# LSH attention with spectral token mixing on Trainium2: q and k handed over transposed, and split without TensorE transposes

## The chip, the cores and the metric

The kernel runs on one core of one Trainium2 chip. The metric is device microseconds of one execution; smaller is better. The kernel before took 851.65 us (median of three runs, 851.07 to 852.93).

## The reference

Two stages follow each other. The first is attention restricted by hash buckets: q and k (4 batches, 8 heads, 768 tokens, 64 dimensions) are projected on 6 random directions, the 6 signs make a bucket number, and a query sees the keys of its own bucket only. The second mixes tokens and channels.

```python
q_bits = (np.einsum('bhsd,dk->bhsk', q, proj) > 0).astype(np.int64)
k_bits = (np.einsum('bhsd,dk->bhsk', k, proj) > 0).astype(np.int64)
mask = q_bucket[:, :, :, None] == k_bucket[:, :, None, :]
scores = scale * np.matmul(q, k.transpose(0, 1, 3, 2))
scores = np.where(mask, scores, -1000000000.0)
scores = scores - np.max(scores, axis=-1, keepdims=True)
attn = np.exp(scores)
attn = attn / (np.sum(attn, axis=-1, keepdims=True) + 1e-09)
x = np.matmul(attn, v)            # then heads side by side: (4, 768, 512)

theta = x @ w_theta
zr, zi = x * np.cos(theta), x * np.sin(theta)
u = x + np.einsum('ts,bsd->btd', w_tok_r, zr) + np.einsum('ts,bsd->btd', w_tok_i, zi)
out = u + np.maximum(u @ w_ch, 0.0)
```

All inputs and the output are float32 as far as this change is concerned.

## The kernel before

**Tokens and tiles.** 768 tokens are 6 blocks of 128. Token p x 6 + t lies on partition p of block t. Two heads (64 dimensions each) share the 128 partitions of a tile, so there are 16 head pairs, four for each batch. The kernel counts attention in 96 steps: 4 batches x 8 heads x 3.

**Precision.** A float32 value is kept as a high half, rounded for TensorE (type fp32r), and a low half, the remainder. `prep_qk` (L562) makes both for q and k of a head pair. It loads the two inputs with tokens on partitions into two tiles nat (L572, two transfers each, one for each head, in pieces of 64 floats). TensorE turns each block of 128 x 128 against the identity (L592); four results fill one shared PSUM bank, pt. From there ScalarE writes the high half into hl (L597) and VectorE the low half (L600). That happens three times for a head pair, with 12 transposes.

**What follows in the head pair.** TensorE multiplies the halves with the split projection (pb, L76), and VectorE turns signs into rows (L626). `assemble` (L665) copies halves and sign rows by DMA from hl and rows into qt and kt (L672 to L681); a score is then the product of 108 rows of the first plane and 97 of the second. The first head of the run is assembled by copies on ScalarE and VectorE instead (L630, L648, L650). `maxima` (L697) computes a first approximation of all scores (sq), VectorE reduces the row maxima (mc, L723), and the row of shifts goes to qt by DMA.

**The step.** For each chunk of 512 scores TensorE computes st, ScalarE the exponential pf (L801) and its 16-bit high part p (L807), GpSimd the remainder (L813, pf minus p), and TensorE multiplies both with the two halves of v into po. VectorE divides and writes x (L856, L862). `prep_v` (L439) prepares the halves of v, for which VectorE and GpSimd read vb (L486 to L493).

**The mixing.** `moe` (L870) runs for a batch beside the attention of the next: x is transposed and split (pt_x, h_x, l_x; L907 to L916), multiplied with w_theta (ps_th), turned to sine and cosine on ScalarE (L973, L974), multiplied with x (f, L985), split into 16-bit halves (L990 to L996), multiplied with the token weights (py), added to x (L1024), transposed and split again (pt_u), multiplied with w_ch (ps_r) and stored (L1031, L1034). The weights are prepared during batch 0: `widened` (L349) and `prep_wtok` (L402), which transposes the token weights (pwt, L424).

**What sets the order.** Each piece of work is an `Op` with a rank (`prio`), the engines that may do it, each with an assumed cost, the operations that it needs, and its slots. `issue_all` (L111) simulates the engines with these costs and writes out one program for each engine: a free engine takes the ready operation of lowest rank, but leaves it alone if one that ranks ahead by more than AHEAD will be ready within HOLD of its duration. Ranks are the step plus a constant: the load of a head pair has QKL, the transposes and splits QK0, the sign products QK1, assembling AS0, the maxima MX0 and MX1, the mixing TH0, TH1, Y0, Y1, YS. Constants with `_0` or `_3` hold for the first or last batch. Where an operation may run on two engines (L996: GpSimd or VectorE), the simulated state decides. All DMAs are issued by SyncE in one queue, in the planned order.

**PSUM.** Eight banks: two for maxima (mx), two for scores (s) and four shared ones (m), for pt, pb, po, the weight transposes and all of the mixing.

Of the kernel before, what the change touches and what calls it, by code (L numbers as in the profile page):

```python
# [14 lines left out]
F32 = mybir.dt.float32  # L15
# [16 lines left out]
def lsh_attention_moe_kernel(ctx: ExitStack, tc: tile.TileContext, q, k, v, proj, w_theta, w_tok_r, w_tok_i, w_ch, aff, out):  # L32
    nc = tc.nc
    PE, ACT, DVE, POOL = nc.tensor, nc.scalar, nc.vector, nc.gpsimd

    B, H, S, D = q.shape
    NB = proj.shape[1]
# [43 lines left out]
    START = {"PE": 1000, "ACT": 1900, "DVE": 1600, "POOL": 2300, "SP": 500}  # L81
    STREAM = {"qktr": 0.5, "xtr": 0.5, "wtr": 0.5, "mtr": 0.3, "vall": 0.3, "vmean": 0.5, "pv": 0.83, "pv4": 0.25, "y": 1.0, "proj": 0.97}
    LAT = {"PE": 220, "ACT": 120, "DVE": 115, "POOL": 140}
# [355 lines left out]
    def prep_v(b, hp, prio):  # L439
        t = {}  # L440
        sv, sm_, sa = Slot("vv"), Slot("m"), Slot("m")
        full = t["full"] = b * NP + hp in FULL
        svb = Slot("vb")
# [50 lines left out]

        def whole(e):
            def go():
                t["vv"] = ap_.tile([P, 2, T, W1], F32, tag=sv.tag, bufs=1, name=f"vw_{b}_{hp}")
                t["vf"] = t["vv"].rearrange("p h t w -> p (h t) w")
                if e == "ACT":
                    ACT.activation(t["vf"][:, :, :D], src(), AF.Copy, scale=sc)  # L500
                else:
                    DVE.tensor_scalar(t["vf"][:, :, :D], src(), sc, None, ALU.mult)
            return go

        def ones_whole():
            POOL.memset(t["vf"][:, :, D : D + 1], ONE)

        def mean():
# [25 lines left out]
        r = op("vscale", prio, on("DVE", 460, scale), [r])  # L534
        if full:
            l1 = a = op("vw", prio, {"ACT": (830, whole("ACT")), "DVE": (480, whole("DVE"))}, [r], [svb, sv])
            o1 = op("vones", prio, on("POOL", 110, ones_whole), [a], [sv])
        else:
            a = op("vv1", prio, on("ACT", 830, high), [r], [svb, sv])
            o1 = op("vones", prio, on("POOL", 110, ones), [a], [sv])  # L540
            l1 = op("vv2", prio, on("DVE", 930, low), [a], [svb, sv])
        b_ = op("va1", prio, on("POOL", 970, s1), [l1], [svb])
# [19 lines left out]
    def prep_qk(b, hp, G, g):  # L562
        t = {}
        sh, sr = Slot("hl"), Slot("rows")
        nats = []
        for i, src in enumerate((q, k)):
            sn = Slot("nat")

            def load(i=i, src=src, sn=sn):
                t["nat", i] = nat = ap_.tile([P, T, 2, D], F32, tag=sn.tag, bufs=1, name=f"nat{i}_{b}_{hp}")  # L570
                for j in range(2):
                    dma(nat[:, :, j, :], src[b, 2 * hp + j].rearrange("(p t) d -> p t d", t=T))  # L572

            nats.append((op("qkload", G + QKL + 0.02 * i, on("SP", [(625, 2.5 * S * D * 4)] * 2, load), slots=[sn]), sn))

        def hf(c):
            return t["hl"][:, c].rearrange("p i n -> p (i n)")

        pr = G + at("QK0", b)
        TC = 4  # L580
        hs, ls = [], []
        for c0 in range(0, 2 * T, TC):
            def chunk(c0=c0):
                sm_ = Slot("m")
                u = {}
                cs = slice(c0 * P, (c0 + TC) * P)

                def tr():
                    u["pt"] = bank(sm_, [P, TC * P], f"pt_{b}_{hp}_{c0}")
                    for n in range(TC):  # L590
                        i, tt = divmod(c0 + n, T)
                        PE.transpose(u["pt"][:, ts(n, P)], t["nat", i][:, tt].rearrange("p h d -> p (h d)"), ident)  # L592

                def high():
                    if "hl" not in t:
                        t["hl"] = ap_.tile([P, 2, 2, S], F32R, tag=sh.tag, bufs=1, name=f"hl_{b}_{hp}")
                    ACT.activation(hf(0)[:, cs], u["pt"], AF.Copy)  # L597

                def low():
                    DVE.tensor_tensor(hf(1)[:, cs], u["pt"], hf(0)[:, cs].bitcast(F32), ALU.subtract)  # L600

                n0, n1 = c0 // T, (c0 + TC - 1) // T
                a = op("qktr", pr, on("PE", 109 * TC, tr), [nats[i][0] for i in range(n0, n1 + 1)], [nats[i][1] for i in range(n0, n1 + 1)] + [sm_])
                hs.append(op("qkh", pr, on("ACT", 495, high), [a], [sm_, sh]))
                ls.append(op("qkl", pr, on("DVE", 600, low), [hs[-1]], [sm_, sh]))

            chunk()

# [158 lines left out]
    def step(g, b, h, blk, mxt, vt, piece):  # L767
# [15 lines left out]
        for c in range(nc_):  # L783
            def chunk(c=c):
# [30 lines left out]
                def pv():  # L815
                    if "acc" not in t:
                        t["acc"] = bank(sm_, [P, T, W1], f"po_{nm}")
                    vv, mt = vt["vv"], vt["mt"]
                    for qi in range(ni):
                        o = t["acc"][:, i0 + qi]  # L820
                        if c == 0:
                            mm(o, mxt["ft"][:, ts(i0 + qi, P)], mt[:, j, :], begin and qi == 0, False)
                        for n in range(kc):
                            tt, col = c * kc + n, ds(n * ni * P + qi * P, P)
                            if vt["full"]:
                                mm(o, u["pf"][:, col], vv[:, j, tt], False, tt == T - 1)
                                continue
# [220 lines left out]
    g = 0  # L1048
# [24 lines left out]
ORD = 1  # L1073
FULL = ()
PSUM = (("mx", 2), ("s", 2), ("m", 4))
# [5 lines left out]
WIN = {"m": 3, "tmp": 3}  # L1081
MX0 = -3.274
MX1 = 0.377
PIECES = [{1: (0, 3)}, {0: (0, 2), 1: (2, 3)}]
PF = 0.16
KA = 0.3
KB = 0.629
KV = 0.583
KN = 0.872
AB = -0.02  # L1090
WTH = 16.607
WTS = 1.058
WC = 28.159
WCS = 0.722
# [6 lines left out]
SEED = 162248  # L1101
TH0_3 = -1.231
TH1_3 = 0.851
Y0_3 = 9.278
YS_3 = 6.0
Y1_3 = 2.611
MX0_0 = -3.0
MX1_0 = 0.377
AS0_0 = -5.618
PV0_0 = -4.074  # L1110
QK0_0 = -6.17
QK1_0 = -5.94
HOLD = 0.3
LATE = 6
WL0 = 22.0
WLS = 3.0
TH0_0 = 0
TH1_0 = 0.82
Y0_0 = 8.904
Y1_0 = 2.702  # L1120
YS_0 = 6.16
AHEAD = 2.0
QKL = -8.933
QK0 = -6.006
QK1 = -5.0
AS0 = -2.867
PV0 = -4.114
LV0 = -4.311
W0 = 0.4
WS = 3.097  # L1130
TH0 = 0.0
TH1 = 0.82
Y0 = 8.904
YS = 6.16
Y1 = 2.702

# [42 lines left out]
```

## Time and profile before

| | |
|---|---|
| timed runs | 851.07, 851.65, 852.93 us |
| span of the profiled execution | 852.6 us |
| instructions | 18177 |
| mean granted TensorE clock | 0.971 |
| DMA | 79350 packets, 79.03 MB |
| GpSimd, remainder p (L813) | 288 operations, 345.4 us |

For the profiled execution the profile gives its span, from the first to the last instruction; that is the time of that execution as far as it can be seen, and it lies inside the range of the timed runs. A line of a group reads: line, engine, operation, output and inputs, shape, count; then busy time in us and the mean of one in ns; then the idle time of the engine just before, and whose end ended it. PE is a matmul or transpose, PEld the loading of its weights, DVE is VectorE, ACT ScalarE, POOL GpSimd, SP SyncE. Matmuls overlap, so a count times the mean is more than the busy time. In a row of stretches stand the stretch, its length, the busy time of each engine with its number of instructions, the granted clock (1.00 is full), the busy share of the DMA engines and GB/s. In the slices, one digit is a fortieth of the span, in tenths.

### The profile page before, as it was taken

What the parts mean: (1) busy time and instruction counts of PE and PEld (TensorE: products, weight loads), DVE (VectorE), ACT (ScalarE), POOL (GpSimd) and SP (SyncE); (2) the same over time, 40 slices, a digit from 0 to 9 for tenths busy, and PEclk for the clock granted to TensorE, in tenths of its full rate; (3) what the DMA queues carried; (4) which work ended last, traced back from release to release, by engine and by line L of the source; (5) the groups of instructions that cost most, each with busy time, mean ns of one, the idle gap of its engine ahead of it and who ended that gap; (6) DMA issues with size and microseconds to landing.
All of it is one profiled execution on the core that took longest, in us unless ns stands there. A gap on an engine that the chain in (4) does not pass through costs nothing.

```text
span 852.6 us, 18177 instructions
## 1 busy us (share of the span) xinstructions
PE 803.6 (94%) x7000; PEld 580.1 (68%) x7000; DVE 550.2 (65%) x982; ACT 528.5 (62%) x917; POOL 455.1 (53%) x494
## 2 busy tenths in 40 slices
PE   4879878899999999999999999999999999998997
PEld 3567666677666677788666767788667766775554
DVE  6999989675888645675875544674786445235522
ACT  3489878687976355577875445577784554657200
POOL 2297784883596364563685454464675462641200
PEclk7699998899999999999999999999999999999999
DMA  8577585643044272461234351561225140000000
GB/s 221 112 235 175 160 218 129 163 98 79 16 120 118 65 166 74 96 139 43 46 89 101 74 118 41 121 136 47 56 61 128 36 91 33 14 13 1 13 25 37
DMA packets 79350, 79.03 MB, mean 93 GB/s; under 512 B 56184, under 2 KB 60472, under 8 KB 79264
## 3 DMA queue, kind: packets, MB, share of 16 engines
q1 hardware_dynamic: 79264, 77.88, 37.3%
q8 instruction: 55, 0.90, 0.4%
q14 instruction: 31, 0.25, 0.1%
HBM read 32.51 MB, written 6.29 MB: 46 GB/s over the span
## 4 chain that ended last, share of the span: by engine, by line
PE 69%; DVE 13%; ACT 11%; issue 3%; POOL 2%; DMA 2%; SPq 0%; ACTq 0%; DVEq 0%; POOLq 0%
PE py L76 19%; PE st L76 12%; PE po L76 10%; PE ps_r L76 8%; PE sq L76 6%; PE ps_th L76 6%; DVE mc L723 4%; PE pb L76 3%; ACT pf L801 2%; PE pt L592 2%; ACT p L807 2%; PE pt_u L907 1%; DVE f L985 1%; DVE wf_t L379 1%; DVE hl L600 1%
## 5 line engine op out<-in xcount | busy, mean ns | idle before, releaser
L813 POOL TENSOR_TENSOR p<-pf,p 128x512 f16<-128x512 f32 x288 | 345.4, 1222 | 225.4 <-ACT p L807 141.5
L801 ACT ACTIVATE pf<-st 128x512 f32<-128x512 f32 x288 | 164.3, 596 | 129.1 <-PE st L76 115.7
L723 DVE TENSOR_REDUCE mc<-sq 128x1 f32<-128x512 f32 (+1 forms) x288 | 191.2, 682 | 56.5 <-PE sq L76 55.5
L76 PE MATMUL py<-z,wtk 128*128 128x512 f16 x864 | 216.6, 381 | 0.5 <-DVE z L996 0.3
L76 PE MATMUL st<-qt,kt 108*128 108x512 f32 (+3 forms) x768 | 194.4, 368 | 9.0 <-ACT pf L801 8.1
L807 ACT ACTIVATE p<-pf 128x512 f16<-128x512 f32 x288 | 172.2, 632 | 12.1 <-PE po L76 9.5
L76 PE MATMUL po<-vv,p 128*128 128x65 f16 (+1 forms) x3456 | 153.0, 194 | 3.6 <-POOL p L813 3.3
L76 PEld LDWEIGHTS <-p 128*128 128x128 f16 x3456 | 130.8, 98 | 37.3 <-issue 17.9
L76 PE MATMUL sq<-kt,qt 108*128 108x256 f32 (+1 forms) x384 | 131.3, 403 | 14.6 <-DVE mc L723 11.6
L76 PEld LDWEIGHTS st<-qt,kt 108*128 108x128 f32 (+1 forms) x768 | 119.1, 192 | 31.6 <-ACT pf L801 19.2
L76 PEld LDWEIGHTS <-wtk 128*128 128x128 f16 x864 | 73.0, 98 | 82.8 <-issue 18.3
L76 PEld LDWEIGHTS sq<-kt,qt 108*128 108x128 f32 x384 | 69.6, 199 | 36.5 <-DVE mc L723 16.7
L996 POOL TENSOR_TENSOR z<-f,z 128x512 f16<-128x512 f32 x38 | 51.0, 1355 | 66.0 <-ACT z L990 53.9
L76 PE MATMUL ps_th<-wth,h_x 128*128 128x512 f32 x192 | 63.9, 415 | 0.4 <-ACT h_x L912 0.4
L76 PE MATMUL ps_r<-wch,h_u 128*128 128x512 f32 x192 | 62.8, 408 | 0.7 <-ACT h_u L912 0.7
L985 DVE SCALAR_TENSOR_TENSOR f<-x,zsc,z 128x512 f32<-128x512 f32 x48 | 53.6, 1156 | 7.1 <-ACT z L973 4.8
L1031 DVE SCALAR_TENSOR_TENSOR x<-ps_r,x 128x512 f32<-128x512 f32 x24 | 16.6, 691 | 63.9 <-PE ps_r L76 63.9
L912 ACT ACTIVATE h_u<-pt_u 128x512 fp32r<-128x512 f32 x24 | 14.4, 598 | 60.1 <-PE pt_u L907 60.1
L1024 DVE SCALAR_TENSOR_TENSOR x<-py,sw,x 128x512 f32<-128x512 f32 x24 | 18.0, 750 | 41.8 <-PE py L76 41.8
L597 ACT ACTIVATE hl<-pt 128x512 fp32r<-128x512 f32 x48 | 27.4, 596 | 28.1 <-PE pt L592 27.8
L600 DVE TENSOR_TENSOR hl<-pt,hl 128x512 fp32r<-128x512 f32 x48 | 31.9, 685 | 19.1 <-ACT hl L597 17.6
L76 PEld LDWEIGHTS ps_th<-wth,h_x 128*128 128x128 f32 x192 | 36.8, 196 | 9.4 <-ACT h_x L912 0.6
(131 smaller groups left out, 986.8 us busy)
## 6 DMA issues: line engine op xcount, KB each, us to landing
qt<-hl SPq DMA_DIRECT2D x31, 384.0 KB
kt<-hl SPq DMA_DIRECT2D x31, 384.0 KB
nat<-in_q_dram SPq DMA_DIRECT2D x32, 192.0 KB
nat<-in_k_dram SPq DMA_DIRECT2D x32, 192.0 KB
vb<-in_v_dram SPq DMA_DIRECT2D x16, 384.0 KB
out_dram<-x SPq DMA_DIRECT2D x24, 256.0 KB
qt<-hl SPq DMA_DIRECT2D x62, 96.0 KB
kt<-hl SPq DMA_DIRECT2D x62, 96.0 KB
```

Of the source, the lines that this page charges most:

```text
L76: PE.matmul(out_, l, r, start=start, stop=stop, skip_group_check=True)
L592: PE.transpose(u["pt"][:, ts(n, P)], t["nat", i][:, tt].rearrange("p h d -> p (h d)"), ident)
L597: ACT.activation(hf(0)[:, cs], u["pt"], AF.Copy)
L600: DVE.tensor_tensor(hf(1)[:, cs], u["pt"], hf(0)[:, cs].bitcast(F32), ALU.subtract)
L723: DVE.tensor_reduce(col()[:, cs], u["sq"], AX.X, ALU.max)
L801: ACT.activation(wide("pf", spf, F32), u["st"], AF.Exp, scale=1.0 / math.sqrt(D))
L807: ACT.activation(o_, u["pf"], AF.Copy)
L813: return lambda: eng.tensor_tensor(wide("p2", sp2, F16), u["pf"], u["p1"], ALU.subtract)
L985: DVE.scalar_tensor_tensor(u["f"], tl[b][:, tt], zsc[:, b : b + 1], t["zw"][r][:, tt], ALU.mult, ALU.mult)
L996: return lambda: eng.tensor_tensor(t["z"][r, 1][:, tt], u["f"], t["z"][r, 0][:, tt], ALU.subtract)
L1024: DVE.scalar_tensor_tensor(tl[b][:, to], res["py"], t["sw"][:, to : to + 1], tl[b][:, to], ALU.mult, ALU.add)
L1031: DVE.scalar_tensor_tensor(tl[b][:, to], r_["ps"], 0.0, tl[b][:, to], ALU.max, ALU.add)
```

## The change

The host now hands over q and k with the 64 dimensions ahead of the tokens, and the tokens in the order that the transposes gave (block by block). A head pair's 128 rows of 768 floats are loaded with one transfer each for q and k, into a tile raw of the size of nat. The halves are made straight from it, for all 768 columns at once: 2 high and 2 low operations for a head pair instead of 3 and 3. A high half may run on ScalarE or VectorE (before: ScalarE), a low half on GpSimd or VectorE (before: VectorE). The 12 transposes of a head pair and the three uses of a shared bank go. The tile is held until its low half is done. A branch for a wider v that was switched off (FULL was empty) is deleted. Most rank constants have new values, HOLD and AHEAD too, so that the order of all work is planned anew.

```diff
-    B, H, S, D = q.shape
+    B, H, D, S = q.shape
...
-            def load(i=i, src=src, sn=sn):
-                t["nat", i] = nat = ap_.tile([P, T, 2, D], F32, tag=sn.tag, bufs=1, name=f"nat{i}_{b}_{hp}")
-                for j in range(2):
-                    dma(nat[:, :, j, :], src[b, 2 * hp + j].rearrange("(p t) d -> p t d", t=T))
...
-                def tr():
-                    u["pt"] = bank(sm_, [P, TC * P], f"pt_{b}_{hp}_{c0}")
-                    for n in range(TC):
-                        i, tt = divmod(c0 + n, T)
-                        PE.transpose(u["pt"][:, ts(n, P)], t["nat", i][:, tt].rearrange("p h d -> p (h d)"), ident)
...
-                    ACT.activation(hf(0)[:, cs], u["pt"], AF.Copy)
...
-                    DVE.tensor_tensor(hf(1)[:, cs], u["pt"], hf(0)[:, cs].bitcast(F32), ALU.subtract)
...
+                def load():
+                    t["raw", i] = ap_.tile([P, S], F32, tag=sn.tag, bufs=1, name=f"raw{i}_{b}_{hp}")
+                    dma(t["raw", i], src[b, 2 * hp : 2 * hp + 2].rearrange("h d s -> (h d) s"))
+
+                def high(e):
+                    def go():
+                        if "hl" not in t:
+                            t["hl"] = ap_.tile([P, 2, 2, S], F32R, tag=sh.tag, bufs=1, name=f"hl_{b}_{hp}")
+                        if e == "ACT":
+                            ACT.activation(t["hl"][:, 0, i], t["raw", i], AF.Copy)
+                        else:
+                            DVE.tensor_copy(t["hl"][:, 0, i], t["raw", i])
+                    return go
+
+                def low(eng):
+                    return lambda: eng.tensor_tensor(t["hl"][:, 1, i], t["raw", i], t["hl"][:, 0, i].bitcast(F32), ALU.subtract)
+
+                a = op("qkload", G + QKL + 0.02 * i, on("SP", [(625, 2 * S * D * 4)], load), slots=[sn])
+                hs.append(op("qkh", pr + QKI * i, pick(g, QKH, {"ACT": (760, high("ACT")), "DVE": (520, high("DVE"))}), [a], [sn, sh]))
+                ls.append(op("qkl", pr + QKI * i, pick(g, QKLO, {"POOL": (1750, low(POOL)), "DVE": (880, low(DVE))}), [hs[-1]], [sn, sh]))
...
-MX0 = -3.274
+MX0 = -3.263
...
-WTH = 16.607
+WTH = 16.998
...
-Y0_3 = 9.278
+Y0_3 = 11.712
...
-QK0_0 = -6.17
+QK0_0 = -7.07
...
-HOLD = 0.3
+HOLD = 0.255
...
-AHEAD = 2.0
+AHEAD = 2.344
-QKL = -8.933
-QK0 = -6.006
-QK1 = -5.0
-AS0 = -2.867
+QKL = -10.187
+QKI = 0.127
+QKH = [(0, 999, ["ACT", "DVE"])]
+QKLO = [(0, 999, ["POOL", "DVE"])]
+QK0 = -5.533
+QK1 = -4.662
+AS0 = -4.539
...
+        if name in "qk":
+            a = a.reshape(b, h, 128, s // 128, d).transpose(0, 1, 4, 3, 2).reshape(b, h, d, s)
```

More of the change, by code (lines that the diff above doesn't have):

```diff
@@ L441, in prep_v @@
         sv, sm_, sa = Slot("vv"), Slot("m"), Slot("m")
-        full = t["full"] = b * NP + hp in FULL
         svb = Slot("vb")
@@ L493, in s2 @@
                 POOL.tensor_tensor(t["vb"][:, :, 0], t["vb"][:, :, 0], t["vb"][:, :, n], ALU.add)
[L495 to L506, printed above, removed]
         def mean():
@@ L534, in prep_v @@
         r = op("vscale", prio, on("DVE", 460, scale), [r])
[L535 to L541, printed above, removed]
+        a = op("vv1", prio, on("ACT", 830, high), [r], [svb, sv])
+        o1 = op("vones", prio, on("POOL", 110, ones), [a], [sv])
+        l1 = op("vv2", prio, on("DVE", 930, low), [a], [svb, sv])
         b_ = op("va1", prio, on("POOL", 970, s1), [l1], [svb])
@@ L564, in prep_qk @@
         sh, sr = Slot("hl"), Slot("rows")
[L565 removed]
+        raws = []
+        hs, ls = [], []
+        pr = G + at("QK0", b)
         for i, src in enumerate((q, k)):
[L567 to L574 removed]
@@ L576, in hf @@
[L576 to L586, printed above, removed]
-                def tr():
-                    u["pt"] = bank(sm_, [P, TC * P], f"pt_{b}_{hp}_{c0}")
-                    for n in range(TC):
-                        i, tt = divmod(c0 + n, T)
[L592 to L607, printed above, removed]
@@ new lines, in part @@
+            def part(i=i, src=src):
+                sn = Slot("nat")
+                def load():
[15 more added lines that the diff above has]
+                ls.append(op("qkl", pr + QKI * i, pick(g, QKLO, {"POOL": (1750, low(POOL)), "DVE": (880, low(DVE))}), [hs[-1]], [sn, sh]))
@@ L609, in prep_qk @@
+            part()
         fs = []
@@ L1081 @@
 WIN = {"m": 3, "tmp": 3}
-MX0 = -3.274
-MX1 = 0.377
+MX0 = -3.263
+MX1 = 0.411
 PIECES = [{1: (0, 3)}, {0: (0, 2), 1: (2, 3)}]
[L1085 to L1090, printed above, removed]
-WTH = 16.607
-WTS = 1.058
-WC = 28.159
+PF = 0.112
+KA = 0.401
+KB = 0.749
+KV = 0.529
+KN = 1.258
+AB = -0.043
+WTH = 16.998
+WTS = 0.232
+WC = 27.543
 WCS = 0.722
@@ L1101 @@
 SEED = 162248
-TH0_3 = -1.231
-TH1_3 = 0.851
-Y0_3 = 9.278
-YS_3 = 6.0
-Y1_3 = 2.611
-MX0_0 = -3.0
-MX1_0 = 0.377
-AS0_0 = -5.618
-PV0_0 = -4.074
-QK0_0 = -6.17
-QK1_0 = -5.94
-HOLD = 0.3
-LATE = 6
[L1115 to L1119, printed above, removed]
-Y1_0 = 2.702
-YS_0 = 6.16
-AHEAD = 2.0
-QKL = -8.933
-QK0 = -6.006
-QK1 = -5.0
-AS0 = -2.867
[L1127 to L1135, printed above, removed]
+TH0_3 = -0.791
+TH1_3 = 0.535
+Y0_3 = 11.712
+YS_3 = 4.023
+Y1_3 = 0.838
+MX0_0 = -3.0
+MX1_0 = 0.299
+AS0_0 = -5.786
+PV0_0 = -4.367
+QK0_0 = -7.07
+QK1_0 = -5.655
+HOLD = 0.255
+LATE = 6
+WL0 = 33.637
+WLS = 3.314
+TH0_0 = -0.032
+TH1_0 = 0.837
+Y0_0 = 8.598
+Y1_0 = 2.702
+YS_0 = 4.448
+AHEAD = 2.344
[6 more added lines that the diff above has]
+AS0 = -4.539
+PV0 = -4.161
+LV0 = -5.392
+W0 = 0.383
+WS = 3.307
+TH0 = 0.02
+TH1 = 0.742
+Y0 = 8.953
+YS = 5.502
+Y1 = 2.736
 _INS = ["q", "k", "v", "proj", "moe_w_theta", "moe_w_tok_r", "moe_w_tok_i", "moe_w_ch"]
```

13 lines of the change are left out of this document (4 added, 9 removed).

## The prediction

> **What bounds the kernel now.** I read in this order: the page's busy times and slices, the busy times cut into three stretches, the chain that ended last in the first stretch and in the rest, and the groups of instructions of the part that is taken out.
>
> ```profile
> span 852.6 us, 18177 instructions
> PE 803.6 (94%) x7000; PEld 580.1 (68%) x7000; DVE 550.2 (65%) x982; ACT 528.5 (62%) x917; POOL 455.1 (53%) x494
> PE   4879878899999999999999999999999999998997
> DVE  6999989675888645675875544674786445235522
> PEclk7699998899999999999999999999999999999999
> ```
>
> ```profile
> 0.00:170.00 170.00, 138.00 (x1283) 105.48 (x1284) 148.00 (x274) 121.84 (x209) 108.66 (x123) 0.89 0.69 176
> 170.00:725.00 555.00, 546.53 (x4946) 398.24 (x4945) 356.41 (x636) 358.91 (x633) 314.99 (x346) 0.99 0.36 85
> 725.00:852.60 127.60, 119.05 (x778) 76.39 (x774) 45.80 (x73) 47.79 (x77) 31.43 (x27) 0.98 0.05 17
> ```
>
> The columns of the second fence are the stretch, its length, the busy time of PE, PEld, DVE, ACT and POOL, the granted clock, the DMA share and GB/s. TensorE was busy 803.6 of 852.6 us, so 49.0 us were idle. Of these, 32.0 us lie in the first 170 us (batch 0, which has no channel or token mixing of an earlier batch to fill TensorE with), 8.5 us in the next 555 and 8.5 us in the last 128. Behind 170 us nothing but TensorE's own work sets the time: the other engines are busy two thirds of it or less. Ahead of 170 us VectorE is the busiest, with 148.0 us. The chain says the same, first for 0 to 170 us and then for 170 to the end:
>
> ```profile
> by line: DVE mc L723 16.0%; issue 7.3%; DVE wf_t L379 5.8%; PE st L76 5.5%; DMA w_t<-in_moe_w_tok_i_dram 5.1%; PE sq L76 4.6%; PE po L76 4.0%; DVE wf_t L370 3.6%; DVE hl L600 3.0%; PE pt L592 2.9%; DVE wf_t L366 2.7%; ACT p L807 2.7%; DVE w
> ```
>
> ```profile
> by line: PE py L76 23.6%; PE st L76 13.4%; PE po L76 11.6%; PE ps_r L76 10.1%; PE ps_th L76 6.9%; PE sq L76 6.5%; PE pb L76 3.4%; ACT pf L801 2.3%; issue 1.6%; PE pt_u L907 1.5%; PE pt L592 1.5%; DVE f L985 1.5%; ACT p L807 1.3%; ACT z L974
> ```
>
> In the front the first entry is VectorE's row maxima; behind it the list is matmuls, one kind after the other. The transposes of q and k (pt, L592) stand in both: 2.9% of 170 us is 4.9 us and 1.5% of 682.6 us is 10.2 us. These 15.1 us are the least that their removal should bring if nothing new comes; their busy time is the most.
>
> **What is taken out.**
>
> ```profile
> L592 PE MATMUL pt<-ident,nat 128*128 128x128 f32 x192 | 30.5, 296 | 7.0 <-POOL mt L517 5.6 <-DMA nat<-in_q_dram 0.8 <-DVE wtk L428 0.6
> L600 DVE TENSOR_TENSOR hl<-pt,hl 128x512 fp32r<-128x512 f32 x48 | 31.9, 685 | 19.1 <-ACT hl L597 17.6 <-DMA ft<-fl 1.0 <-DMA out_dram<-x 0.4
> L597 ACT ACTIVATE hl<-pt 128x512 fp32r<-128x512 f32 x48 | 27.4, 596 | 28.1 <-PE pt L592 27.8
> ```
>
> ```profile
> 0.00:20.00 20.00, 3.90 (x16) 3.00 (x16) 1.98 (x3) 1.79 (x3) 0.80 0.89 223
> 20.00:45.00 25.00, 2.18 (x8) 1.58 (x8) 1.99 (x3) 1.77 (x3) 0.68 0.51 112
> 45.00:85.00 40.00, 1.50 (x12) 1.29 (x12) 1.89 (x3) 1.55 (x3) 1.00 0.77 213
> 85.00:130.00 45.00, 1.47 (x12) 1.34 (x12) 1.87 (x3) 1.57 (x3) 0.98 0.69 181
> 130.00:170.00 40.00, 2.91 (x16) 2.19 (x16) 2.04 (x3) 1.70 (x3) 0.84 0.61 149
> 170.00:200.00 30.00, 1.23 (x8) 0.93 (x8) 1.97 (x3) 1.70 (x3) 0.96 0.34 78
> 200.00:852.60 652.60, 17.34 (x120) 14.28 (x120) 20.18 (x30) 17.27 (x30) 0.99 0.30 72
> ```
>
> The second fence holds the instructions that touch pt alone: PE, PEld, DVE, ACT. There are 192 transposes, 12 for each of 16 head pairs, in 30.5 us; one takes 296 ns from start to end, but they overlap, so the price is 17.34 / 120 = 0.145 us in the dense part. Behind 170 us they take 1.23 + 17.34 = 18.6 us, ahead of it 3.90 + 2.18 + 1.50 + 1.47 + 2.91 = 12.0 us.
>
> *Behind 170 us* TensorE is full (546.53 of 555.00 us), so I take the whole 18.6 us. The bounds are 10.2 us, the chain's share, and 18.6 us.
>
> *Ahead of 170 us* the places differ:
>
> ```profile
> 20.00:45.00 25.00, 21.18 (x106) 15.53 (x106) 24.29 (x48) 11.54 (x21) 7.42 (x12) 0.68 0.51 112
> 45.00:130.00 85.00, 71.16 (x815) 55.74 (x815) 79.22 (x132) 71.59 (x121) 68.01 (x65) 0.99 0.73 196
> 130.00:170.00 40.00, 36.46 (x332) 28.01 (x332) 31.64 (x57) 30.96 (x62) 28.37 (x31) 0.84 0.61 149
> 160.00:170.00 10.00, 8.33 (x54) 6.19 (x55) 4.47 (x8) 5.22 (x11) 8.70 (x10) 0.61 0.81 191
> ```
>
> ```profile
> 5.62 1.10 PE pt L592 x4
> ...
> 10.63 1.29 DVE hl L600 x2
> ...
> 115.98 8.63 DMA w_t<-in_moe_w_tok_i_dram
> ```
>
> In the head, four transposes stand on the chain with 1.10 us and fall out: 1.1 us. From 20 to 130 us VectorE is full (24.29 of 25 and 79.22 of 85 us), so what counts there is VectorE's low halves, 1.99 + 1.89 + 1.87 = 5.75 us for three head pairs, and where their replacement runs. From 130 to 170 us TensorE is at 36.46 of 40 us, so 2.91 x 0.91 = 2.6 us come back.
>
> **What is put in.** For each of 32 tiles, now 768 wide and read from SBUF, one high half on ScalarE or VectorE and one low half on GpSimd or VectorE.
>
> ```profile
> L648 ACT ACTIVATE kt<-hl x1: 841/841/841, 12.2 to 12.2; 32x768 fp32r<-32x768 f32 x1
> L486 DVE SCALAR_TENSOR_TENSOR vv<-vb,vsc,vv x16: 999/1252/1935, 23.0 to 693.4; 128x768 f16<-128x768 f32 x16
> L813 POOL TENSOR_TENSOR p<-pf,p x288: 1147/1164/2718, 40.4 to 759.8; 128x512 f16<-128x512 f32 x144
> L600 DVE TENSOR_TENSOR hl<-pt,hl x48: 669/681/693, 7.4 to 679.7; 128x512 fp32r<-128x512 f32 x48
> L996 POOL TENSOR_TENSOR z<-f,z x38: 1153/1250/1611, 211.9 to 796.7; 128x512 f16<-128x512 f32 x38
> L996 DVE TENSOR_TENSOR z<-f,z x10: 675/724/1427, 213.0 to 795.9; 128x512 f16<-128x512 f32 x10
> ```
>
> High halves: the same copy of 768 took 841 ns on ScalarE, so all 32 there are 26.9 us against 27.4 us before. Price nothing; ScalarE is at 62%. If that cover were gone, each would hold up a row of exponentials by 0.84 - 0.60 = 0.24 us, 8 us in all.
>
> Low halves: the operation of 768 with two SBUF operands took 1.25 us (median) on VectorE; on GpSimd I estimate 1.164 x 768 / 512 = 1.75 us from the row of 512. The planner already has such a choice in L996, and gave 38 of 48 to GpSimd. With that split, of the six low halves between 20 and 130 us about 1.3 fall on VectorE, 1.6 us in place of 5.75: VectorE is relieved by 4.1 us and I take these. All six on VectorE would be 7.5 us, a loss of 1.8 us; all on GpSimd is 10.5 us more on an engine with 68.01 of 85 us, so up to 5.75 us of gain. I take 4.1 because L996 is the same choice made by the same rule. In the whole run GpSimd gets 25 x 1.75 = 44 us more.
>
> A low half on GpSimd stands ahead of the remainder p (L813) on the same engine, and the PV matmuls wait for p.
>
> ```profile
> POOL p L813 <- ACT p L807: 141.5, 56, 12.7
> PE po L76 <- POOL p L813: 3.3, 4, 1.1
> ```
>
> GpSimd itself waits 141.5 us for work, and TensorE waited for it only 3.3 us in the run. I price the delay at nothing: the cover is the other matmuls in TensorE's queue. Without it, half a low half (0.9 us) for each of 25 gives 22 us, the far end.
>
> Loads: 64 transfers in pieces of 256 bytes become 32 in rows of 3072 bytes.
>
> ```profile
> L572 SPq DMA_DIRECT2D nat<-in_q_dram x32: 584/636/1434, 0.7 to 632.2; - x32
> SPq L572 <- PE pt L592: 26.1, 5, 11.3
> ```
>
> SyncE gets 32 issues fewer of about 0.64 us, 20 us on a queue that is not on the chain. The tile is now free only after the low half, not after the transposes, so the queue may wait longer at this place (it waited 26.1 us for pt), and the copies to qt and kt stand behind it. The due times put the load 10.187 - 5.533 = 4.7 steps ahead of the split and 1.3 steps, some 12 us, behind the split of the pair before it (a step is 852.6 / 96 = 8.9 us): cover enough for the 1.75 us low half. I price loads at nothing both ways; what they could give is a share of the 8.63 us wait for w_t in the quoted chain.
>
> PSUM: 48 uses of a shared bank go. Only who waits for banks gains, and behind 170 us that is inside the 8.5 us of idle time; nothing is taken. The new ranks move the order everywhere. Their cost has no row; its bounds are the idle time that a better order can remove (half of the front's 32 us, 16 us) and as much in the other direction; I take zero.
>
> **The sum.** 18.6 + 1.1 + 4.1 + 2.6 = 26.4 us. 852.6 - 26.4 = 826.2 us of span. The page gives no time outside the span; its 852.6 stands 0.95 us above the median of the timed runs (851.65) and inside them. Less that, 825.3, so 825 us.
>
> **The rivals.** *The front gives nothing back.* There the chain runs through row maxima, weight preparation and the w_t transfer, none of which changes. For it: VectorE's share of the chain, and 5.1% for the transfer. Against it: hl on VectorE has 3.0% of that chain and pt 2.9%. 852.6 - 18.6 - 1.1 = 832.9, so 832 us.
>
> *VectorE and GpSimd hold each other up.* The old low half read one operand from PSUM and never varied (669 to 693 ns); those with both operands in SBUF range from 999 to 1935 ns and 675 to 1427 ns. If each of the six early ones takes the 1.935 us on VectorE, that is 11.6 in place of 5.75 us, a loss of 5.9 us, and the front gives 1.1 + 2.6 - 5.9 = -2.2 us. GpSimd's p reached 2.718 us against 1.164, 1.55 us more; over the 26 later ones that is 40 us on GpSimd, of which I let TensorE feel an eighth, 5 us. 852.6 - 18.6 + 2.2 + 5 = 841.2, so 840 us. Against it: L996 has its typical 724 ns near its least. The Trainium skill, "SBUF — State Buffer", section "Who interferes with whom", says that a VectorE instruction with two SBUF inputs and a GpSimd instruction that reads SBUF exclude each other, and one with at most one SBUF input does not; by that rule this case would come about whenever the two meet. The trace agrees in the spread of these rows (669 to 693 against 999 to 1935 ns), not yet in the price.
>
> *The new order also removes idle time.* The front has 32.0 us of it. All transposes (30.5) and a quarter of that idle time (8 us) gone: 814.1, so 813 us. For it: fewer steps compete for VectorE and for the four shared banks. Against it: the w_t wait stays.
>
> *Slower: the clock falls in batch 0's stage.* From 160 to 170 us TensorE was busy 8.33 of 10 us and still had only 0.61 of its clock. From 45 to 130 us it is busy 84%, and without the transposes 80%. If the whole stretch from 45 to 170 us ran at 0.61, its work, (71.16 - 2.97) x 0.99 / 0.61 + (36.46 - 2.91) x 0.84 / 0.61 = 157 us, would outlast the 125 us by 32: 852.6 - 18.6 - 1.1 + 32 = 865, so 864 us. It turns slower from a mean clock of 0.66 in this stretch on. Against it: the same stretch holds 0.99 at 84% now. The Trainium skill, "TensorE: Matmul & The Clock Gate", section "Part 4: PE-mode transpose", says that transposes do not count as activity for the gate; by it their removal leaves the clock where it is, and this case falls away. No row here separates transposes from matmuls in that respect.
>
> That the transposes stay in some form cannot be: the new code has no such instruction for q and k.
>
> **How the numbers follow.** Forecast (818 to 829) 0.48; front gives nothing (829 to 836) 0.17; mutual hold-up (836 to 848) 0.12; idle time gone too (805 to 818) 0.16; clock 0.03; other orders that cost the whole gain 0.04, of which half end within 0.2% (1.7 us, about what a measurement here tells from no change). Faster 0.93, same 0.02, slower 0.05. The range 812 to 840 leaves out some of the best case (0.06), half of the hold-up case (0.06) and the last two (0.07), 0.19 in all.
>
> **What would show it.** The chain reaches the first long group of batch 0's mixing here:
>
> ```profile
> 190.14 5.70 PE ps_th L76 x24
> ```
>
> Right: TensorE's busy time near 773 us with no pt of q and k; idle time near 53 us; TensorE from 170 us on as full as before; the first ps_th group (190.14 us) some 8 us earlier; VectorE's total lower by 20 us or more, GpSimd's higher by about 44. The splits at 0.84, 1.25 and 1.75 us. Wrong: a first stretch as long as before, low halves mostly on VectorE near 1.9 us, waits of po for p above 10 us, a granted clock under 0.8 from 45 to 130 us, or idle time above 20 us behind 170.

## The result, and the profile after

The changed kernel is slower: 856.51 us (median of 7 runs, 854.09 to 857.69) beside 851.86 us for the kernel before on the same chip. The ratio is 1.0052, with a 95% interval of 1.0033 to 1.0071, so 4.4 us were lost where 26.4 were forecast to be won. The profiled execution lasted 855.4 us.

First the page of the kernel after: span, busy times, and the slices of TensorE, VectorE and the granted clock.

```profile
span 855.4 us, 17719 instructions
PE 794.8 (93%) x6808; PEld 566.4 (66%) x6808; DVE 570.4 (67%) x962; ACT 520.9 (61%) x888; POOL 497.1 (58%) x511
PE   3799988899898899999999999999999999999997
DVE  7999988786898755575896455575796445235413
PEclk8599996979899999999999999999999999999999
```

The transposes are gone: 192 matmuls fewer, 30.5 us of busy time. Yet TensorE is busy only 8.8 us less (803.6 to 794.8). Matmuls overlap: in the kernel before, the other 6808 matmuls cover 785.4 us by themselves, so that the transposes had TensorE to themselves for 18.2 of their 30.5 us only, and the same 6808 matmuls now take 9.4 us more. Its idle time is 855.4 - 794.8 = 60.6 us against 49.0. VectorE was to be relieved and has 20.2 us more; GpSimd has 42.0 us more. The clock is 0.954 over the run, before 0.971.

The kernel after by stretches (columns as before: PE, PEld, DVE, ACT, POOL, clock, DMA):

```profile
0.00:170.00 170.00, 134.37 (x1235) 102.43 (x1235) 148.34 (x266) 118.68 (x199) 119.91 (x128) 0.86 0.63 172
170.00:725.00 555.00, 537.79 (x4762) 385.77 (x4763) 374.43 (x623) 349.52 (x607) 343.83 (x356) 0.97 0.36 85
725.00:855.40 130.40, 122.64 (x813) 78.22 (x811) 47.66 (x74) 52.72 (x84) 33.33 (x28) 1.00 0.05 19
```

The chain that ended last, by line, first from 0 to 170 us, then from 170 us to the end:

```profile
by line: DVE mc L691 12.1%; PE st L76 10.2%; PE po L76 6.6%; PE sq L76 6.0%; issue 5.7%; DVE hl L569 5.1%; POOL p L781 4.5%; DVE wtk L428 4.3%; PE pwt L424 3.4%; DMA w_th<-in_moe_w_theta_dram 3.1%; SPq L644 2.7%; DVE wf_t L379 2.6%; DVE wf_
```

```profile
by line: PE py L76 23.0%; PE st L76 12.5%; PE po L76 10.2%; PE ps_r L76 10.1%; PE sq L76 6.3%; PE ps_th L76 5.7%; PE pb L76 2.9%; issue 2.6%; ACT pf L769 2.2%; ACT p L775 1.7%; POOL p L781 1.5%; PE pt_u L870 1.5%; DVE mc L691 1.3%; DVE hl L
```

The pt entries have left the chain, but VectorE's share for hl in the front rose from 3.0% to 5.1% of 170 us (5.1 to 8.7 us), and GpSimd's p stands in it with 4.5%. Behind 170 us the low half of hl now stands in the part of the list that is shown.

The splits themselves, from the tile raw (count, then least, median and greatest ns, then first and last start):

```profile
L563 ACT ACTIVATE hl<-raw x22: 825/842/891, 3.9 to 661.8; 128x768 fp32r<-128x768 f32 x22
L569 DVE TENSOR_TENSOR hl<-raw,hl x18: 945/1525/2593, 4.8 to 662.4; 128x768 fp32r<-128x768 f32 x18
L569 POOL TENSOR_TENSOR hl<-raw,hl x14: 1805/2119/3060, 5.9 to 662.7; 128x768 fp32r<-128x768 f32 x14
L565 DVE CAST hl<-raw x10: 538/560/1396, 23.8 to 661.8; 128x768 fp32r<-128x768 f32 x10
```

The high half on ScalarE hardly varies. The low half on VectorE takes anything from 945 to 2593 ns, the one on GpSimd 1805 to 3060. Two other rows stretched with them. The remainder p on GpSimd (after):

```profile
L781 POOL TENSOR_TENSOR p<-pf,p 128x512 f16<-128x512 f32 x288 | 357.6, 1263 | 193.5 <-ACT p L775 118.6 <-issue 50.0 <-PE st L76 9.4
```

It was 345.4 us. And the product f on VectorE, which reads x and z, first before, then after:

```profile
L985 DVE SCALAR_TENSOR_TENSOR f<-x,zsc,z x48: 739/865/1654, 210.4 to 794.3; 128x512 f32<-128x512 f32 x48
```

```profile
L948 DVE SCALAR_TENSOR_TENSOR f<-x,zsc,z x48: 736/1628/2318, 211.6 to 798.5; 128x512 f32<-128x512 f32 x48
```

The median of f nearly doubles; its busy time in all rises less, from 53.6 to 58.9 us.

Where in the run the loss arises shows when the exponentials (pf, 288 in all) are taken as milestones. The busy time of ScalarE in pf alone, with the count of pf, before and then after:

```profile
0.00:182.00 182.00, 41.09 (x72) 0.89 0.67 172
182.00:376.50 194.50, 43.98 (x74) 1.00 0.38 92
376.50:759.00 382.50, 86.92 (x148) 1.00 0.32 74
```

```profile
0.00:182.60 182.60, 40.73 (x72) 0.84 0.61 167
182.60:387.50 204.90, 43.84 (x74) 0.97 0.37 92
387.50:762.00 374.50, 87.25 (x148) 0.99 0.32 75
```

(The counts include a few table loads.) The same work ended at 182.6 instead of 182.0 us, so the front gave nothing. The next part, batch 1's attention beside batch 0's mixing, took 204.9 instead of 194.5 us. The last part won back 382.5 - 374.5 = 8.0 us. In the middle part the granted clock was 0.97, before 1.00, so 0.03 x 204.9 = 6 us of clock were not granted; how much of the 10.4 us lost there that makes up is not shown. The chain of the kernel after shows what else stands there:

```profile
206.84 1.25 SPq L643
208.08 0.04 issue
208.13 1.84 SPq L644
...
213.52 1.67 DMA ft<-fl
...
215.60 0.83 ACT hl L563
216.43 0.02 issue
216.45 1.28 ACT L769
217.74 0.60 ACT pf L769
```

SyncE's issues of the copies to qt and kt (L643, L644) end the chain here for several us, then a high half and a table load stand on ScalarE ahead of the exponential that TensorE needs. The first long ps_th group, which was forecast 8 us earlier, starts 3.5 us later than 190.14:

```profile
193.65 5.73 PE ps_th L76 x24
```

### The profile page after: what moved, and what is told of

It is laid out like the page before. It is cut to its first block, busy times and chain, and to the rows that moved or that the text cites. A ratio compares the mean times of both kernels' runs of the same rounds, so it can differ in the third digit from the quotient of the medians.

```text
span 855.4 us, 17719 instructions
## 1 busy us (share of the span) xinstructions
PE 794.8 (93%) x6808; PEld 566.4 (66%) x6808; DVE 570.4 (67%) x962; ACT 520.9 (61%) x888; POOL 497.1 (58%) x511
## 4 chain that ended last, share of the span: by engine, by line
PE 65%; DVE 14%; ACT 9%; SPq 3%; issue 3%; DMA 3%; POOL 3%; DVEq 0%; ACTq 0%; POOLq 0%
PE py L76 18%; PE st L76 12%; PE po L76 9%; PE ps_r L76 8%; PE sq L76 6%; PE ps_th L76 5%; DVE mc L691 3%; PE pb L76 2%; POOL p L781 2%; ACT pf L769 2%; DVE hl L569 2%; ACT p L775 2%; PE pt_u L870 1%; SPq L644 1%; SPq L643 1%
## 5 line engine op out<-in xcount | busy, mean ns | idle before, releaser
L781 POOL TENSOR_TENSOR p<-pf,p 128x512 f16<-128x512 f32 x288 | 357.6, 1263 | 193.5 <-ACT p L775 118.6
L76 PE MATMUL py<-z,wtk 128*128 128x512 f16 x864 | 222.4, 385 | 1.2 <-POOL z L959 0.8
L76 PE MATMUL st<-qt,kt 108*128 108x512 f32 (+3 forms) x768 | 201.1, 378 | 8.1 <-ACT pf L769 7.9
L76 PEld LDWEIGHTS <-p 128*128 128x128 f16 x3456 | 136.4, 100 | 44.9 <-issue 19.0
L76 PE MATMUL po<-vv,p 128*128 128x65 f16 (+1 forms) x3456 | 158.3, 197 | 6.2 <-POOL p L781 6.1
L76 PE MATMUL sq<-kt,qt 108*128 108x256 f32 (+1 forms) x384 | 137.4, 415 | 21.0 <-DVE mc L691 14.7
L948 DVE SCALAR_TENSOR_TENSOR f<-x,zsc,z 128x512 f32<-128x512 f32 x48 | 58.9, 1266 | 9.9 <-ACT z L936 7.3
L76 PEld LDWEIGHTS ps_r<-wch,h_u 128*128 128x128 f32 x192 | 35.5, 191 | 9.6 <-ACT h_u L875 0.9
L76 PE MATMUL ps_th<-wth,l_x 128*128 128x512 f32 x96 | 38.9, 406 | 0.1
L76 PE MATMUL ps_r<-wch,l_u 128*128 128x512 f32 x96 | 38.3, 399 | 0.0
```

The lines of the kernel that those rows point to most:

```text
L76: PE.matmul(out_, l, r, start=start, stop=stop, skip_group_check=True)
L781: return lambda: eng.tensor_tensor(wide("p2", sp2, F16), u["pf"], u["p1"], ALU.subtract)
L948: DVE.scalar_tensor_tensor(u["f"], tl[b][:, tt], zsc[:, b : b + 1], t["zw"][r][:, tt], ALU.mult, ALU.mult)
```

## The experiments

Four theories were tested; the expectations use their names. *Port*: VectorE and GpSimd hold each other up, because the low halves no longer read PSUM but two operands in SBUF. *Queue*: the loaded tile is held until the low half, the next load waits for it in SyncE's queue, and the copies to qt and kt stand behind. *Clock*: TensorE is granted less clock. *Order*: the new ranks or the new plan cost it. "The old order" is the kernel before with the same instructions in the same order on every engine, apart from those named; its 48 low and 48 high halves become 64 each, because a chunk is cut at the border of q and k. A difference in us between two experiments is the difference of their ratios to the kernel before times 852, with their intervals combined as a root of squares.

### In the old order, piece by piece

**old_order_no_tr**: q and k handed over transposed, halves split from the loaded tiles, no transposes, nothing else moved.

```diff
-                        PE.transpose(u["pt"][:, ts(n, P)], ...)
+                    pass
...
-                    ACT.activation(hf(0)[:, cs], u["pt"], AF.Copy)
+                    for i, lo, hi in runs:
+                        ACT.activation(t["hl"][:, 0, i, lo:hi], t["nat", i][:, lo:hi], AF.Copy)
...
-                    DVE.tensor_tensor(hf(1)[:, cs], u["pt"], hf(0)[:, cs].bitcast(F32), ALU.subtract)
+                    for i, lo, hi in runs:
+                        DVE.tensor_tensor(t["hl"][:, 1, i, lo:hi], t["nat", i][:, lo:hi], ..., ALU.subtract)
```

> The order of the kernel before on every engine, unchanged; q and k come transposed, the 192 transposes of q and k are left out, and the halves of q and k are split from the loaded tiles on the same engines in the same places (ScalarE, VectorE; the middle piece in two operations). If the new order lost what the removal gives (theory order): 826 to 836 us. If the removal itself closes the clock gate or leaves TensorE waiting (theory clock): 846 to 858 us, with more than 60 us at half clock. If two operands from SBUF on VectorE cost it (theory port): 836 to 848 us, with the low halves near 1.0 us for 512 columns instead of 0.68 us.

Measured 872.85 us, 1.0243 [1.0211, 1.0274], above all three ranges.

**old_order_tr_idle**: the same, but the transposes still run and nobody reads them (`PE.transpose` put back).

> As the kernel before in every order, transposes kept as ballast (their result is not read), halves split from the loaded tiles. It prices the SBUF source alone. Theory order and theory clock: within 3 us of the kernel before. Theory port: 8 to 20 us slower than it.

Measured 870.5 us, 1.0227 [1.0196, 1.0257]. Taking the transposes out of this order is worth nothing that could be measured (1.4 +- 3.7 us to the bad), and reading the loaded tiles costs 2%.

**old_order_low_psum**: transposes run, the high half comes from the loaded tile, the low half reads the bank again; one SBUF operand, as in the kernel before. The bank holds blocks that do not match the high half, so the low half keeps its cost, but what it writes is not the remainder.

```diff
-    DVE.tensor_tensor(t["hl"][:, 1, i, lo:hi], t["nat", i][:, lo:hi], ..., ALU.subtract)
+    DVE.tensor_tensor(t["hl"][:, 1, i, lo:hi], u["pt"][:, p0 : p0 + hi - lo], ..., ALU.subtract)
```

> The order of the kernel before with transposes kept, high half read from the loaded tile, but the low half reads its minuend from PSUM again (the transposes' result, which here is not the right number: the low halves are left out in effect). One operand from SBUF instead of two; the tile is free early again. Theory port: 848 to 855 us, against 870.5 us with both operands in SBUF; low halves again 0.68 us. If it stays above 862 us the port is not the cause in the old order.

Measured 853.16 us, 1.0016 [0.9994, 1.0038]: all of the loss is gone. The low halves of the two kernels, old_order_tr_idle first:

```profile
L603 DVE TENSOR_TENSOR hl<-nat,hl x64: 407/680/2749, 7.0 to 692.9; 128x512 fp32r<-128x512 f32 x32, 128x256 fp32r<-128x256 f32 x32
```

```profile
L604 DVE TENSOR_TENSOR hl<-pt,hl x64: 406/547/692, 6.8 to 678.3; 128x512 fp32r<-128x512 f32 x32, 128x256 fp32r<-128x256 f32 x32
```

The least time is the same, so a second SBUF operand as such costs nothing here. Only the long ones differ.

**old_order_low_two**: as old_order_low_psum, but both operands are the high half in SBUF, so that it writes zeros. The tile is free as early as there.

```diff
-    DVE.tensor_tensor(t["hl"][:, 1, i, lo:hi], u["pt"][:, p0 : p0 + hi - lo], ..., ALU.subtract)
+    DVE.tensor_tensor(t["hl"][:, 1, i, lo:hi], t["hl"][:, 0, i, lo:hi].bitcast(F32), t["hl"][:, 0, i, lo:hi].bitcast(F32), ALU.subtract)
```

> The same instructions in the same order on every engine as old_order_low_psum (853.2 us), transposes kept as ballast; the low half's first operand is now the high half in SBUF instead of the PSUM bank (the low half is zero in effect). Against old_order_tr_idle (870.5) the tile of q or k is free at the split, not after the low half. Theory port (two SBUF operands on VectorE are the price): 864 to 872, low halves from 0.4 to over 2 us in place of 406 to 692 ns. Rival queue (the price is the tile held until the low half): 852 to 855, though the rows may stretch.

Measured 862.72 us, 1.0129 [1.0114, 1.0144], between the two theories. *Port* is worth 9.6 +- 2.3 us, and 8.3 +- 2.9 us remain up to old_order_tr_idle. Its low halves:

```profile
L603 DVE TENSOR_TENSOR hl<-hl x64: 406/681/2741, 6.9 to 688.0; 128x512 fp32r<-128x512 f32 x32, 128x256 fp32r<-128x256 f32 x32
```

VectorE is busy with them for 55.9 us, in old_order_low_psum for 33.9. The traces also show beside what they stretch. In old_order_low_two, the 33 low halves that no GpSimd instruction overlapped for 50 ns or more took 411 to 692 ns; the other 31 have medians of 1407 ns (512 columns) and 1290 ns (256 columns). In old_order_low_psum the overlapped ones took 406 to 692 ns, like the rest.

For the rest of the loss, SyncE's waits at the load show what differs, in old_order_low_two and then in old_order_tr_idle (total us, times, longest):

```profile
SPq L572 <- PE pt L593: 39.9, 14, 11.1
SPq L572 <- ACT hl L599: 11.8, 14, 1.8
```

```profile
SPq L572 <- DVE hl L603: 82.0, 24, 13.4
```

**old_order_no_tr_late** and **old_order_tr_late**: the loads of the next pair issued behind the copies to qt and kt instead of ahead of them, without and with transposes.

```diff
             def load(i=i, src=src, sn=sn):
+                if b or hp:
+                    pending.append(lambda: fetch(i, src, sn))
...
                 dma(kf[D : D + hd, c], hk()[h0 + c * hd : h0 + (c + 1) * hd, 0])
+            flush("copies")
```

> The order of the kernel before without transposes (872.9 us with loads in their old place), now with the loads behind the copies to qt and kt. Theory queue: 845 to 858 us. Theory port: 866 to 876 us.

> As old_order_tr_idle (870.5 us; the order of the kernel before, transposes as ballast, halves split from the loaded tile), but with the loads behind the copies to qt and kt, so that SyncE's queue does not wait for low halves. What is left above the kernel before is the second operand from SBUF alone. Theory port: 862 to 870 us. If the tile that is held longer is the cause: 851 to 857 us.

Measured 866.6 us, 1.0184 [1.0141, 1.0227], which is in the range of *port*, and 872.69 us, 1.0234 [1.0211, 1.0257], which is above both ranges. Without transposes the later load gives 5.0 +- 4.5 us, about the remainder above. With them it gives nothing, but there the late load makes TensorE wait for its data (pt, 11.6 us). So in the old order *queue* has a share, which these runs bound only roughly.

**old_order_one_tr**: old_order_low_psum with one transpose a chunk instead of four; the low half reads that block four times. It takes 144 of the 192 transposes away and gives nobody a second SBUF operand.

```diff
-                    for n in range(TC):
+                    for n in range(1):
...
+    DVE.tensor_tensor(..., u["pt"][:, None, :P].to_broadcast([P, m, P]), ..., ALU.subtract)
```

> old_order_low_psum (853.2 us) with one transpose in each chunk in place of four; the low half reads that one block four times from PSUM (its values are left wrong in effect). 144 of 192 transposes go, nothing gets a second SBUF operand. If TensorE's time counts in the old order as well as in the new one, 3/4 of the 12.6 us: 843 to 845. If transposes are hidden in the old order (old_order_no_tr gained nothing over old_order_tr_idle): 852 to 854.

Measured 850.66 us, 0.9986 [0.9971, 1.0000], between the two ranges: 2.6 +- 2.2 us are won. The stretches ahead of and behind 170 us, old_order_low_psum first:

```profile
0.00:170.00 170.00, 140.44 (x1315) 107.10 (x1315) 150.35 (x282) 124.02 (x217) 110.89 (x123) 0.95 0.65 175
170.00:851.60 681.60, 664.25 (x5685) 472.84 (x5685) 403.50 (x717) 405.90 (x717) 346.23 (x372) 0.99 0.29 72
```

```profile
0.00:170.00 170.00, 135.50 (x1238) 101.11 (x1239) 147.48 (x280) 122.55 (x214) 108.83 (x122) 0.95 0.64 172
170.00:847.90 677.90, 653.98 (x5619) 460.69 (x5617) 405.06 (x719) 406.67 (x720) 347.78 (x373) 1.00 0.29 73
```

TensorE's busy time fell by 804.69 - 789.49 = 15.2 us, and the span by 3.7; 11.5 us turned into idle time. At 664 of 682 us busy behind 170 us, TensorE's work alone did not set the time.

### In the new order

**new_order_plus_tr**: the kernel after with 12 transposes for each pair, read by nobody, ahead of the sign products.

```diff
+                    for n in range(6):
+                        i = n % 2
+                        PE.transpose(u["pb"][:, ts(n // 3, P)], t["hl"][:, 0, i, ts(n, P)].bitcast(F32), ident)
```

> The changed kernel in its own order, with 12 transposes for each head pair put back as ballast ahead of the sign products (result not read). It prices TensorE's part in the new order. Theory order: 10 to 20 us slower than the changed kernel (856.5), 866 to 877 us, since TensorE bounds the later two thirds. Theory clock: within 5 us of the changed kernel, or faster, 850 to 861 us, with less half-clock time. Theory port: 868 to 877 us.

Measured 869.11 us, 1.0197 [1.0161, 1.0232]: 12.4 +- 3.4 us more than the kernel after. Here transposes do cost time, though these read the halves and stand behind the split, not ahead of it as in the kernel before.

**new_order_low_zero**: the low half is left out; its engine fills the place with zeros instead.

```diff
-return lambda: eng.tensor_tensor(t["hl"][:, 1, i], t["raw", i], t["hl"][:, 0, i].bitcast(F32), ALU.subtract)
+return lambda: eng.memset(t["hl"][:, 1, i].bitcast(F32), 0.0)
```

> The changed kernel in its own order with each low half of q and k replaced by filling it with zeros on the same engine in the same place: the low halves are left out; nothing is read from SBUF and the raw tile is free after the high half. It gives what the low halves cost the new order in all. Theory port and theory queue: 828 to 842 us. Theory order (the planned order itself, whatever the low halves take): 850 to 857 us.

Measured 841.29 us, 0.9868 [0.9829, 0.9906]: 15.7 +- 3.7 us less. A fill takes 698 ns on VectorE and 734 to 749 ns on GpSimd, so this is not the whole of the low halves. It holds their own time, the hold-up and the longer hold of the tile together; this run does not split them. In size it makes up for the 12.4 us that the transposes are worth in this order.

**new_order_late_load**: loads behind the copies, the same edit as above.

> The changed kernel, every engine's order unchanged, but in the SyncE queue the loads of a head pair's raw tiles stand behind the copies to qt and kt of the pair before instead of ahead of them, so that a load that waits for a low half holds up less. Theory queue (loads that wait in SyncE's queue for low halves, 82.7 us in all, delay the copies behind them): 838 to 848 us. Theory port (low halves with two operands from SBUF and GpSimd's work hold each other up): within 4 us of the changed kernel, 852 to 860 us.

Measured 859.47 us, 1.0101 [1.0070, 1.0132], 4.2 +- 3.1 us more than the kernel after, though the load's waits for low halves (67.1 + 15.6 us of SyncE's time) are gone. *Queue* falls for the new order.

**new_low_pool**: all high halves on ScalarE, all low halves on GpSimd (QKH and QKLO), planned anew.

> The changed kernel with every high half on ScalarE and every low half on GpSimd, planned anew with the new ranks. VectorE loses the 28.0 us of low and the high halves it had, GpSimd gets about 32 us more. Theory port (VectorE's operations with two operands from SBUF are what costs): 838 to 850 us. If GpSimd's low halves cost as much (they stand ahead of p, and hold VectorE's f and vv up): 852 to 862 us.

Measured 863.3 us, 1.0123 [1.0086, 1.0160]. VectorE is relieved (570.4 to 554.4 us), GpSimd loaded (497.1 to 517.1), and it is 6.0 +- 3.5 us slower, above both ranges. In this one plan, moving the whole to GpSimd is no way out.

### The ranks and the plan

**path_old_ranks** is the kernel after with the constants of before; **ranks_only** the kernel before with the constants of after. Both are planned anew.

> The changed kernel with all rank constants of the kernel before, planned anew. Theory order: 826 to 838 us. Theory clock: 848 to 860 us. Theory port: 838 to 852 us.

> The kernel before, transposes and all, with the new ranks. If the new ranks are worse by themselves: 858 us or more. If they are no worse (theory port): 846 to 856 us.

Measured 857.89 us, 1.0084 [1.0057, 1.0112], which is in the range written down for *clock*, and 869.31 us, 1.0200 [1.0183, 1.0218]. The new ranks are not what loses: on the new path they are 2.7 +- 2.8 us better than the old ones, on the old path 17 us worse.

**new_shared**: "qkl" is added to the planner's list of operations that exclude each other between VectorE and GpSimd. **old_ranks_shared** is the same edit under the old ranks.

```diff
-    SHARED = {"p1", "p2", "zf", "zh", "zl", "mag", "wlow", "whigh", "wmul", "wl", "vv2"}
+    SHARED = {"p1", "p2", "zf", "zh", "zl", "mag", "wlow", "whigh", "wmul", "wl", "vv2", "qkl"}
```

> The changed kernel, planned anew with the low halves named among the operations for which the planner lets VectorE and GpSimd exclude each other (before, it did not know that of them). If the plan's ignorance of the exclusion costs the time: 840 to 851 us. If the exclusion costs it whatever the plan knows: 852 to 860 us.

> path_old_ranks (857.9 us) with the low half of q and k in the planner's list of operations that exclude each other between VectorE and GpSimd, planned anew. If the planner's ignorance costs as in the new ranks (856.5 to 849.4): 849 to 852. If the 7 us were an accident of that one plan: 856 to 860 or anywhere within the spread that before_jit1 shows.

Measured 849.38 us, 0.9970 [0.9954, 0.9985], and 871.74 us, 1.0233 [1.0211, 1.0255]. The first beats both kernels, by 7.0 +- 2.1 us the kernel after. But the same edit under the old ranks loses 12.7 +- 3.0 us. So the 7 us are not shown to be the work of the exclusion in the plan; they may be the luck of one plan.

**before_jit1**, **before_jit2**, **after_jit1**: ranks disturbed at random by up to 0.05 of a step, which also breaks their ties in another order (JIT = 0.05, SEED 1 or 2).

> The kernel before with its ranks disturbed by up to 0.05 of a step and planned anew: how much time hangs on the exact plan alone. If plans this near to each other are equal: 850 to 854. If the plan is finely set: 856 to 870, and then differences of under 10 us between two plans say little of a mechanism.

> The kernel before with its ranks disturbed by up to 0.05 of a step, another draw than before_jit1 (889.6 us). If nearly every plan near the old one is that much slower: 875 to 895. If before_jit1 was an unlucky draw: 850 to 865.

> The changed kernel with its ranks disturbed by up to 0.05 of a step and planned anew. If the new plan is as finely set as the old one (before_jit1 lost 38 us): 880 to 900. If before's plan was the rarer one and after's is an ordinary plan of its kind: 856 to 870; then part of the missing gain is the plan and not the data path.

Measured 889.62 us, 1.0441 [1.0419, 1.0463]; 894.2 us, 1.0484 [1.0448, 1.0519]; 898.36 us, 1.0540 [1.0498, 1.0583]. A plan this near costs 38 and 41 us on the old path, 42 on the new one; the first lies above both of its ranges. As far as three draws tell, both kernels' plans are set equally finely. So each run that was planned anew (new_low_pool, path_old_ranks, ranks_only and the two with the exclusion) tells of one plan, not of its ranks or engines in general.

### The account

In ratios to the kernel before: tiles in the new layout, loaded by rows, and high halves from SBUF, +0.2% (within its interval); second SBUF operand, +1.1%; tile read until the low half, +1.0%; transposes out, +0.2% (nothing); that is 1.0243, in the old order. Planning anew, with the choice of engines and 768 columns at once, takes back 1.6%; the new ranks 0.3%, and 1.0052 is left. These last two are what single plans gave, and why they give it is not shown. In the order of the changed kernel itself the balance is alike: 12.4 +- 3.4 us for the transposes on one side, 15.7 +- 3.7 us for the low halves on the other.

*Clock* does not order the times: the profiles of old_order_low_psum and old_order_tr_late show 0.983 and 0.978 at 853.16 and 872.69 us, and that of new_order_low_zero 0.965 at 841.29. But a share in the changed kernel's loss is not excluded. Its seven executions were granted 0.954 to 0.968, and its profile leaves (1 - 0.954) x 855.4 = 39 us of clock not granted, the one before (1 - 0.971) x 852.6 = 25 us.

## Why the prediction was wrong

**The step that failed first: "TensorE is full (546.53 of 555.00 us), so I take the whole 18.6 us."** Two things in it were wrong. The term was too large from the start: the 18.6 us are the time in which any transpose ran, and other matmuls ran beside it. From 170 to 725 us the other matmuls of the same trace cover 537.4 of the 546.5 us, so the transposes alone had 9.2 us (as far as the modelled ends of matmuls tell). The sign "busy time near 773 us" took all 30.5 us off in the same way. And the busy share was read as a bound. In the old order, 144 of 192 transposes took 15.2 us of busy time away and gave 2.6 +- 2.2 us, where three quarters of the terms 18.6, 1.1 and 2.6 are 16.7 us; the rest became idle time. Even the lower bound, 10.2 us from the chain's share, did not hold there. A reading that fits, but that no run isolates: the other chains are as long as TensorE's here, so that work taken out at one place leaves a gap. In the new order 192 transposes cost 12.4 us; that is two thirds of 18.6 and was the part of the forecast nearest to right. That the idle time is nowhere near 0 was to be seen; that it would grow was not asked. It grew from 17.0 to 25.0 us behind 170 us, beyond the 20 us that the prediction named as a sign of being wrong.

**The second: "VectorE is relieved by 4.1 us and I take these."** The sign was wrong. The busy time of the splits alone (tile raw) from 20 to 130 us in the kernel after, for VectorE, ScalarE and GpSimd:

```profile
20.00:130.00 110.00, 7.52 (x5) 3.34 (x4) 6.18 (x3) 0.86 0.63 174
```

VectorE has three low halves (5.94 us) and two high ones (1.58), 7.52 us in place of 5.75. The planner gave GpSimd 14 of 32 low halves, not the 79% that L996 suggested, and 10 of 32 high halves came to VectorE. Each low half on VectorE took 1.56 us in the mean, not 1.25, and on GpSimd 2.16, not 1.75. In all, VectorE has 28.0 + 8.2 us for splits where it had 31.9.

**The rival that came about** is *VectorE and GpSimd hold each other up*, given 0.12 and 840 us. Its mechanism is shown in the old order: the same operation in the same place ranges to 692 ns with one SBUF operand and to 2741 ns with two, the long ones are those beside GpSimd's work, and 9.6 +- 2.3 us hang on the operand alone. This is what the Trainium skill, "SBUF — State Buffer", section "Who interferes with whom", says of a VectorE instruction with two SBUF inputs beside a GpSimd instruction that reads SBUF; the trace agrees (up to 692 ns alone, a median of 1407 ns beside GpSimd, for 512 columns). In the changed kernel the hold-up is a part of the 15.7 us that is not measured apart. Its own sum was too mild. It began from the 18.6 us that were never there in full, and it put what holds TensorE up behind 170 us at 5 us. Its sizes for the rows were not too small: p took 12.2 us more in all, where 40 were allowed. The stretch of f, which it did not name, is for the larger part not the low halves' doing: with fills in their place (new_order_low_zero) f still has a median of 1416 ns and takes 56.8 us in all, against 53.6 before and 58.9 after, and in old_order_low_two it keeps its old median (864 ns). That part goes with the new plan.

**"Loads ... at nothing both ways."** In the old order the longer hold has a share of up to 8.3 us; in the new order a later load gains nothing, so for the changed kernel nothing speaks against the term. **High halves at nothing**: right in size (842 ns on ScalarE), but those that came to VectorE put 8.2 us there. **"The new ranks ... I take zero"**: right for what the ranks weigh on the new path (2.7 +- 2.8 us), but the plan as a whole was not priced: orders from nearly the same ranks lie 38 us apart.

*The front gives nothing back* came true as well (182.0 to 182.6 us for the same 72 exponentials). *The clock falls in batch 0's stage* did not: 45 to 130 us ran at 0.93 (before 0.99) and 130 to 170 us at 0.84 as before, not at 0.66. The Trainium skill, "TensorE: Matmul & The Clock Gate", section "Part 4: PE-mode transpose", has transposes not count for the clock; new_order_plus_tr with its 192 more was granted 0.955 to 0.967 in four executions, the kernel after 0.954 to 0.968 in seven, which agrees but proves little.

What stays open: why the same 6808 matmuls took 9.4 us more of TensorE's busy time (the lower clock is a candidate), how the 8.3 us divide between the hold of the tile and the plan around it, and what part of the low halves' 15.7 us in the changed kernel is hold-up. Low halves that read one SBUF operand without a transpose weren't tried.

## What to carry to other kernels

A busy share of 98% was not a bound here, and the busy time of a group counts what runs beside other work, too: take a piece of the work out in the same order (old_order_one_tr is such a test) before its time is counted as won. When an operand moves from PSUM to SBUF, price the instruction as such instructions run beside GpSimd in the trace (here 1407 ns in the median against 681), not at the typical time of a row that rarely meets it. And where a plan is written out by a simulation, compare data paths in one fixed order: two plans from nearly the same ranks differed here by more than the change.

## What the runs showed of the hardware

- Two SBUF operands cost a VectorE subtraction nothing by themselves (least 407 against 406 ns), but up to four times its length beside GpSimd's work (2749 against 692 ns greatest; the 33 of 64 that GpSimd didn't overlap stayed at 692 ns or less). GpSimd's own subtraction of 768 columns ranged from 1805 to 3060 ns.
- Adding 192 transposes to the new order brought 21.5 us more busy time and 16.1 us of span in the profiled executions; taking 144 from the old order took 15.2 us of busy time and 3.7 of span.
- SyncE issues a transfer of 128 rows of 3072 bytes in 334 to 354 ns (median), the old one in pieces of 64 floats in 636 to 640 ns. A transfer of 64 rows of 3072 bytes (old_order_no_tr) took 563 to 576 ns, so the size of the piece is not the whole of it.
